# Merging 64-row tails into 128-row blocks and pinning TensorE to program order in a fused attention, Fourier-mixing and MLP kernel

## The chip, the cores and the metric

One core of a Trainium2 chip. The metric is device microseconds (us) of one execution. Every execution told of here was in the fast state (granted TensorE clock 0.968 to 0.985 over the whole span). Each variant ran four times, interleaved on the same chip with runs of the kernel before; different sets of variants ran on different chips, where the kernel before had medians of 1899.0 to 1903.5 us. Between sets, ratios compare better than medians. "Profile" and "trace" are one recorded execution of a kernel.

## The reference, cut to what matters

```python
def _attn_ref(q, k, v, tau):                       # q, k, v: (8, 8, 576, 64) fp32
    scores = np.matmul(q, k.transpose(0, 1, 3, 2)) / np.sqrt(64)
    thresh = np.max(scores, axis=-1, keepdims=True) - tau
    scores = np.where(scores >= thresh, scores, -1e9)
    attn = np.exp(scores - np.max(scores, axis=-1, keepdims=True))
    return np.matmul(attn / (attn.sum(-1, keepdims=True) + 1e-9), v)

def _moe_ref(x, w_ch1, w_ch2):                     # x: (8, 576, 512), the heads side by side
    u = x + np.real(np.fft.fft(np.fft.fft(x, axis=1), axis=2))
    un = (u - u.mean(-1)) / np.sqrt(u.var(-1) + 1e-6)          # cut: keepdims
    return u + np.maximum(un @ w_ch1, 0.0) @ w_ch2  # 512 -> 2048 -> 512
```

## The kernel before: the parts that matter

A batch is four pairs of heads. A pair is five steps of queries: four of 128 rows and a tail of 64 (576 = 4 x 128 + 64). A step computes scores (`sc`, two heads in the two row halves of the array), a reduction, an exponential and a masked product on VectorE and ScalarE, then transposes of the weights (`pw`) and of their last columns and the reciprocals (`pe`). After five steps `weighted_values` (`pv`) follows. Between these pieces `fill()` puts work of earlier batches: Fourier mixing (`py`, `pa`) and MLP (`ph`, `po`, `pn`). This filling is what keeps TensorE busy.

The "array shape" of a matmul is the part of TensorE's array that it uses, rows by columns; the traces print it, as 64*128 for scores or 128*128 for a full transpose. Two matmuls in a row with different ones make a "change of shape".

```python
ROWS = [128, 128, 128, 128, 64]
def prep_pair(n):                       # q and k of a pair to [head_dim, rows]
    for src, tag in ((qt, "qT"), (kt, "kT")):
        pt = ps.tile([128, 1024], FP32, tag="wide", bufs=3, name="pt")
        for t in range(NT):
            m = ROWS[t]
            nc.tensor.transpose(pt[:, 128 * t : 128 * t + m], src[0:m, t, :, :], ident[0:m, 0:m])
        # ... to qT on VectorE, to kT on ScalarE
def scores(i):
    sc = [ps.tile([128, 2, 512], FP32, tag="wide", bufs=3, name=f"sc{j}") for j in range(2)]
    for c in range(2):
        for j in range(2):
            hp = slice(64 * j, 64 * j + 64)
            nc.tensor.matmul(sc[j][0:m, c, 0:HALF], qT[hp, 128 * t : 128 * t + m],
                             kT[hp, HALF * c : HALF * (c + 1)], start=True, stop=True)
    # ... per head: neg (max), e (exp), e * (sc >= thr) with its sum; then rec = 1 / sum
def transposed_weights(i):
    pw = ps.tile([128, 8, 128], FP32, tag="wide", bufs=3, name="pw")   # 8 transposes of e
    nc.scalar.copy(e_t[:, :, qs], pw[:, :, 0:m])
    pe = ps.tile([128, 4, 128], FP32, tag="mm", name="pe")             # 2 transposes
    nc.scalar.copy(ends[:, :, qs], pe[:, 0:2, 0:m])
def weighted_values(n):
    for h in range(2):
        pv = ps.tile([128, 512], FP32, tag="mm", name="pv")            # 10 matmuls
        nc.vector.tensor_tensor(out=x[:, cols], in0=pv[:, 0:HALF], in1=ends[:, 1, cols], op=ALU.mult)
    # ... x, with two rows swapped by DMA, is folded on GpSimd: half, then f
    if n % NPAIR == 1:
        fold_chunks(b, 1)                                              # two sums of f on VectorE
# the loop
for i in range(total + 1):
    if i < total: scores(i)
    fill()
    if i > 0: transposed_weights(i - 1)
    if t == 3: prep_pair(n + 1)         # cut: not for the last pair
    fill()
    if i > 0 and t == 0: weighted_values(n - 1)
    # ... queue the mixing and the MLP groups of a finished batch
    fill()
for unit in mixes + [unit for _, unit in work]:
    for _ in unit: pass
```

PSUM has two kinds of buffers here: three "wide" ones of 1024 values a row (`sc`, `pt`, `pw`) and two small "mm" ones of 512 (`pe`, `pv`, `py`, `pa`, `ph`, `po`, `pn`). A scheduler orders each engine's instructions when the program is built; it may place a matmul ahead of another that was written earlier. "Pinning" below means that TensorE keeps the order of the program text instead.

Of the kernel before, what the change touches and what calls it, by code (L numbers as in the profile page):

```python
# [9 lines left out]
FP32 = mybir.dt.float32  # L10
INT32 = mybir.dt.int32
UINT32 = mybir.dt.uint32
ALU = mybir.AluOpType
ACT = mybir.ActivationFunctionType
# [33 lines left out]
def kernel(  # L48
# [12 lines left out]
    nc = tc.nc  # L61
# [2 lines left out]
    HID = w_ch1.shape[1]  # L64
    assert S == 576 and D == 64 and DM == 512 and H % 2 == 0
    NPAIR = H // 2
    ROWS = [128, 128, 128, 128, 64]
    NT = len(ROWS)
    ND = DM // 128
    NJ = HID // 128  # L70
    HALF = S // 2
# [38 lines left out]
    def load_pair(n):  # L110
        b, p = n // NPAIR, PAIRS[n % NPAIR]
        hs = [2 * p + (j + p) % 2 for j in range(2)]
        qt = sb.tile([128, NT, 2, D], FP32, tag="q", bufs=1, name="q_in")
        kt = sb.tile([128, NT, 2, D], FP32, tag="k", bufs=1, name="k_in")
        for j, h in enumerate(hs):
            nc.sync.dma_start(
                out=qt[:, 0:4, j, :], in_=q[b, h, 0:512, :].rearrange("(t p) d -> p t d", p=128)
            )
            nc.sync.dma_start(out=qt[0:64, 4, j, :], in_=q[b, h, 512:576, :])


        h = hs[0]
        nc.sync.dma_start(
            out=kt[:, 0:4, 0, :], in_=k[b, h, 0:512, :].rearrange("(t p) d -> p t d", p=128)
        )
        nc.sync.dma_start(out=kt[0:64, 4, 0, :], in_=k[b, h, 512:576, :])
        h = hs[1]
        nc.sync.dma_start(out=kt[0:64, 0, 1, :], in_=k[b, h, 512:576, :])
        rows = k[b, h, 0:512, :].rearrange("(t r p) d -> p r t d", r=2, p=64)
        nc.sync.dma_start(out=kt[64:128, 0:4, 1, :], in_=rows[:, 0])  # L130
        nc.sync.dma_start(out=kt[0:64, 1:5, 1, :], in_=rows[:, 1])
        loaded[n] = (qt, kt)

    def load_v(n):

# [189 lines left out]

    def prep_pair(n):

        qt, kt = loaded.pop(n)
        ts = []
        for src, tag in ((qt, "qT"), (kt, "kT")):  # L330
            pt = ps.tile([128, 1024], FP32, tag="wide", bufs=3, name="pt")
            for t in range(NT):
                m = ROWS[t]
                nc.tensor.transpose(  # L334
                    pt[:, 128 * t : 128 * t + m], src[0:m, t, :, :], ident[0:m, 0:m]
                )
            dst = sb.tile([128, S], FP32, tag=tag, name=tag)
            if tag == "qT":
                nc.vector.tensor_scalar(
                    out=dst[:, :], in0=pt[:, 0:S], scalar1=q_scale[:, :], scalar2=None, op0=ALU.mult  # L340
                )
            else:
                nc.scalar.copy(dst[:, :], pt[:, 0:S])
            ts.append(dst)
        heads[n] = (ts[0], ts[1], v_in[n % 2])
        if n + 1 < B * NPAIR:
            load_pair(n + 1)

    def scores(i):
        n, t = divmod(i, NT)  # L350
        qT, kT = heads[n][0:2]
        m = ROWS[t]
        sc = [ps.tile([128, 2, 512], FP32, tag="wide", bufs=3, name=f"sc{j}") for j in range(2)]
        for c in range(2):
            for j in range(2):
                hp = slice(64 * j, 64 * j + 64)
                nc.tensor.matmul(  # L357
                    sc[j][0:m, c, 0:HALF],
                    qT[hp, 128 * t : 128 * t + m],
                    kT[hp, HALF * c : HALF * (c + 1)],  # L360
                    start=True,
                    stop=True,
                )
        neg = sb.tile([128, 2], FP32, tag="neg", bufs=3, name="neg")
        thr = sb.tile([128, 2], FP32, tag="thr", bufs=3, name="thr")
        den = sb.tile([128, 2], FP32, tag="den", bufs=3, name="den")

        e = sb.tile([128, 2 * S], FP32, tag="e", name="e")
        for j in range(2):
            nc.vector.tensor_reduce(  # L370
                out=neg[0:m, j : j + 1], in_=sc[j][0:m, :, 0:HALF], axis=AXIS_XY, op=ALU.max,
                negate=True,
            )
        nc.vector.tensor_scalar(
            out=thr[0:m, :], in0=neg[0:m, :], scalar1=-1.0, scalar2=thr_off[0:m, :],
            op0=ALU.mult, op1=ALU.add,
        )
        for j in range(2):
            ej = e[0:m, S * j : S * (j + 1)].rearrange("p (c n) -> p c n", c=2)
            nc.scalar.activation(  # L380
                out=ej, in_=sc[j][0:m, :, 0:HALF], func=ACT.Exp, bias=neg[0:m, j : j + 1], scale=1.0
            )
            nc.vector.scalar_tensor_tensor(  # L383
                out=ej, in0=sc[j][0:m, :, 0:HALF], scalar=thr[0:m, j : j + 1], in1=ej,
                op0=ALU.is_ge, op1=ALU.mult, accum_out=den[0:m, j : j + 1],
            )
        nc.vector.tensor_scalar(
            out=den[0:m, :], in0=den[0:m, :], scalar1=1e-9, scalar2=None, op0=ALU.add
        )
        nc.vector.reciprocal(den[0:m, :], den[0:m, :])  # L390
        rec = sb.tile([128, 2 * D], FP32, tag="rec", name="rec")
        nc.gpsimd.tensor_copy(  # L392
            rec[0:m, :].rearrange("p (j d) -> p j d", j=2), _repeated(den[0:m, :], D)
        )
        steps[i] = (e, rec)

    def transposed_weights(i):
        n, t = divmod(i, NT)
        m = ROWS[t]
        e, rec = steps.pop(i)  # L400
        if t == 0:


            e_t = sb.tile([128, 8, S], FP32, tag="e_t", bufs=1, name="e_t")
            ends = sb.tile([128, 2, S], FP32, tag="ends", bufs=1, name="ends")
            vt = heads[n][2]
            if PAIRS[n % NPAIR] % 2:

                vt = sb.tile([128, 10, D], FP32, tag="vr", bufs=1, name="v_rev")
                src = heads[n][2]  # L410
                nc.gpsimd.tensor_copy(vt[:, :, 0:1], src[:, :, 0:1])
                last = src[:, :, D - 1 : D]
                down = bass.AP(
                    tensor=last.tensor, offset=last.offset,
                    ap=[list(last.ap[0]), list(last.ap[1]), [-1, D - 1]],
                )
                nc.gpsimd.tensor_copy(vt[:, :, 1:D], down)
            heads[n] = (*heads[n][0:2], vt, e_t, ends)
        e_t, ends = heads[n][3:5]
        qs = slice(128 * t, 128 * t + m)  # L420
        pw = ps.tile([128, 8, 128], FP32, tag="wide", bufs=3, name="pw")
        for j in range(2):
            for c in range(4):
                c0 = (S + D) * j + 128 * c
                nc.tensor.transpose(  # L425
                    pw[:, 4 * j + c, 0:m], e[0:m, c0 : c0 + 128], ident[0:m, 0:m]
                )
        nc.scalar.copy(e_t[:, :, qs], pw[:, :, 0:m])  # L428
        pe = ps.tile([128, 4, 128], FP32, tag="mm", name="pe")
        nc.tensor.transpose(pe[:, 0, 0:m], e[0:m, 512:640], ident[0:m, 0:m])  # L430
        nc.tensor.transpose(pe[:, 1, 0:m], rec[0:m, :], ident[0:m, 0:m])  # L431
        nc.scalar.copy(ends[:, :, qs], pe[:, 0:2, 0:m])  # L432

    def weighted_values(n):

# [68 lines left out]
    def mixing(b):  # L504
# [15 lines left out]
                out=out_, in0=in0, scalar=factor, in1=in1, op0=ALU.mult, op1=ALU.add  # L520
            )
        nc.vector.tensor_tensor(out=f[:, 0, O], in0=s01[:, 0, O], in1=s01[:, 1, O], op=ALU.subtract)
        yield 0
        yield 0

        COS = ((0, 0, 65), (1, 65, 129), (2, 129, 257))
        SIN = ((0, 0, 128), (3, 128, 256))
# [160 lines left out]
    total = B * per_batch  # L688
    groups = 0
    todo = 0.0  # L690
    for i in range(total + 1):
        if i < total:
            scores(i)
        fill()
        n, t = divmod(i, NT)
        if i > 0:
            transposed_weights(i - 1)
        if t == 3 and n + 1 < B * NPAIR:
            prep_pair(n + 1)
        fill()  # L700
        if i > 0 and t == 0:
            weighted_values(n - 1)
            if n + 1 < B * NPAIR:
                load_v(n + 1)
        for _ in itertools.islice(chunks, 2):
            pass
        if i == 2:
            load_dim()
            load_seq()
        if i > 0 and i % per_batch == 0:  # L710
            b = i // per_batch - 1
            mixes.append(mixing(b))
            todo += MIX
            while (groups + 1) * GT <= (b + 1) * S:
                work.append((b, channels(groups)))
                groups += 1
                todo += GROUP
            keep = 0.25 * GROUP
            per_slot = (todo - spent - keep) / (3 * per_batch)
            budget = spent  # L720
        fill()
    for unit in mixes + [unit for _, unit in work]:
        for _ in unit:
            pass


# [44 lines left out]
```

## Time and profile before

1902.98 us, median of three runs (1898.41 to 1903.65). I divide a trace into three stages, which the rest of the text uses: batch 0, to the first score matmul of batch 1; the middle, to the last weighted-values matmul; the drain, to the end.

| kernel before | us |
|---|---|
| span of the trace | 1898.7 |
| batch 0 / middle / drain | 197.8 / 1494.6 / 206.4 |
| TensorE / VectorE / ScalarE / GpSimd busy | 1813.0 / 890.6 / 610.4 / 280.5 |
| waits of TensorE after 260 us, sum | 21 |
| changes of shape in the middle | 620 |

The rows that carry the argument stand in the prediction below. One more, the chain of waits: followed back from the last instruction, it stays on TensorE for 84 of 100 parts of the span. Of VectorE's 163 us on it, 89 lie in batch 0 and 71 are spread over the middle.

```profile
PE 84%; DVE 9%; POOL 3%; ACT 1%; issue 1%; SPq 1%; DMA 1%; DVEq 0%; POOLq 0%; ACTq 0%
```

### The profile page before, as it was taken

To read this page: it belongs to the slowest core of one execution; us is meant where nothing else is said; L and a number is where in the kernel's file an instruction comes from. 1 tells how busy PE (TensorE), PEld (TensorE's weight loads), DVE (VectorE), ACT (ScalarE), POOL (GpSimd) and SP (SyncE) were. 2 spreads that over 40 slices of the span, in tenths; PEclk is the share of its full clock that TensorE was granted. 3 is DMA by queue.
4 is the path that set the end of the run, shared out by engine and by line. 5 is a ranking of instruction groups with operands and counts; after the bars stand their busy time and mean duration, and the time that the engine had idled before them with its cause. 6 is when DMAs were issued, how large, how long until landed. Compare 5 with 4: busy or idle time off the path is not lost.

```text
span 1898.7 us, 21358 instructions
## 1 busy us (share of the span) xinstructions
PE 1813.0 (95%) x7920; PEld 1012.1 (53%) x7920; DVE 890.6 (47%) x2072; ACT 610.4 (32%) x1110; POOL 280.5 (15%) x568
## 2 busy tenths in 40 slices
PE   6777899999999999999999999999999999999999
PEld 3444655555455555555555555555555555555454
DVE  6998745543343555553344445544333355541010
ACT  3555534233223334332223234322323233421010
POOL 4444111121101021102011021102011021101000
PEclk9876999999999999999999999999999999999999
DMA  5432100100001110110000110101000001000000
GB/s 154 128 113 81 32 18 15 37 24 7 19 25 26 29 26 14 31 31 7 19 24 13 30 26 14 34 22 25 13 23 20 22 23 25 1 12 6 11 6 17
DMA packets 129803, 57.00 MB, mean 30 GB/s; under 512 B 120642, under 2 KB 120643, under 8 KB 129700
## 3 DMA queue, kind: packets, MB, share of 16 engines
q1 hardware_dynamic: 129588, 55.38, 10.9%
q8 instruction: 63, 1.03, 0.2%
q14 instruction: 40, 0.33, 0.1%
q0 software_dynamic: 112, 0.26, 0.1%
HBM read 46.02 MB, written 9.44 MB: 29 GB/s over the span
## 4 chain that ended last, share of the span: by engine, by line
PE 84%; DVE 9%; POOL 3%; ACT 1%; issue 1%; SPq 1%; DMA 1%; DVEq 0%; POOLq 0%; ACTq 0%
PE po L645 27%; PE ph L624 25%; PE sc L357 11%; PE pv L446 9%; PE pw L425 6%; PE pt L334 2%; DVE neg L370 2%; DVE e L383 2%; PE py L533 1%; POOL u_t L572 1%; POOL u_t L576 1%; PE pe L430 1%; DVE stage L279 1%; PE pa L550 1%; PE pe L431 1%
## 5 line engine op out<-in xcount | busy, mean ns | idle before, releaser
L624 PE MATMUL ph<-u_t,w 128*128 128x384 f32 x1536 | 533.6, 496 | 10.2 <-POOL u_t L572 4.7
L645 PE MATMUL po<-w,h 128*128 128x512 f32 x1152 | 536.3, 603 | 0.0
L380 ACT ACTIVATE e<-sc,neg 128x576 f32<-128x576 f32 (+1 forms) x320 | 230.0, 740 | 598.7 <-DVE neg L370 598.5
L624 PEld LDWEIGHTS ph<-u_t,w 128*128 128x128 f32 x1536 | 282.1, 191 | 214.3 <-issue 23.7
L370 DVE TENSOR_REDUCE neg<-sc 128x1 f32<-128x576 f32 (+1 forms) x320 | 230.4, 750 | 308.0 <-PE sc L357 307.5
L645 PEld LDWEIGHTS po<-w,h 128*128 128x128 f32 x1152 | 204.8, 190 | 228.8 <-issue 225.1
L357 PE MATMUL sc<-kT,qT 64*128 64x288 f32 (+1 forms) x1280 | 268.7, 450 | 37.8 <-DVE e L383 16.9
L383 DVE SCALAR_TENSOR_TENSOR e<-sc,thr,e 128x576 f32<-128x576 f32 (+1 forms) x320 | 250.7, 814 | 31.9 <-ACT e L380 14.7
L357 PEld LDWEIGHTS sc<-kT,qT 64*128 64x128 f32 (+1 forms) x1280 | 133.8, 183 | 167.5 <-issue 87.8
L392 POOL COPY rec<-den 128x128 f32<-128x128 f32 (+1 forms) x160 | 49.7, 311 | 1127.5 <-DVE den L390 842.1
L428 ACT COPY e_t<-pw 128x1024 f32<-128x1024 f32 (+1 forms) x160 | 148.0, 925 | 145.5 <-PE pw L425 140.2
L425 PEld LDWEIGHTS pw<-ident,e 128*128 128x128 f32 (+1 forms) x1280 | 143.3, 146 | 70.9 <-issue 49.2
L425 PE MATMUL pw<-ident,e 128*128 128x128 f32 (+1 forms) x1280 | 166.3, 274 | 0.5 <-DVE e L383 0.3
L630 ACT ACTIVATE h<-ph 128x384 f32<-128x384 f32 x96 | 47.1, 490 | 331.3 <-PE ph L624 331.3
L632 DVE TENSOR_SCALAR h<-ph 128x384 f32<-128x384 f32 x96 | 53.3, 555 | 201.7 <-PE ph L624 201.5
L451 DVE TENSOR_TENSOR x<-pv,ends 128x288 f32<-128x288 f32 x64 | 29.3, 458 | 178.5 <-PE pv L446 178.5
L652 DVE SCALAR_TENSOR_TENSOR u<-po,rstd,u 128x512 f32<-128x512 f32 x36 | 27.0, 749 | 127.2 <-PE po L645 127.2
L446 PE MATMUL pv<-e_t,v_in 128*64 128x288 f32 x512 | 71.9, 417 | 0.0
L446 PE MATMUL pv<-e_t,v_rev 128*64 128x288 f32 x512 | 71.4, 418 | 0.2 <-ACT ends L432 0.2
L432 ACT COPY ends<-pe 128x256 f32<-128x256 f32 (+1 forms) x160 | 57.1, 357 | 0.9 <-PE pe L431 0.8
L446 PEld LDWEIGHTS pv<-e_t,v_in 128*64 128x64 f32 x512 | 35.6, 138 | 37.4 <-issue 7.4
L446 PEld LDWEIGHTS pv<-e_t,v_rev 128*64 128x64 f32 x512 | 35.4, 139 | 36.2 <-issue 10.5
(123 smaller groups left out, 1335.8 us busy)
## 6 DMA issues: line engine op xcount, KB each, us to landing
stage<-in_moe_w_ch_dram SPq DMA_DIRECT2D x32, 512.0 KB, 4.1
out_dram<-u SPq DMA_DIRECT2D x36, 256.0 KB, 2.0
q_in<-in_q_dram SPq DMA_DIRECT2D x64, 128.0 KB, 2.4
v_in<-in_v_dram SPq DMA_DIRECT2D x64, 128.0 KB, 2.4
k_in<-in_k_dram SPq DMA_DIRECT2D x32, 128.0 KB, 2.4
k_in<-in_k_dram SPq DMA_DIRECT2D x64, 64.0 KB, 2.3
q_in<-in_q_dram SPq DMA_DIRECT2D x64, 16.0 KB, 2.2
k_in<-in_k_dram SPq DMA_DIRECT2D x64, 16.0 KB, 2.1
```

The source lines that it names most:

```text
L357: nc.tensor.matmul(sc[j][0:m, c, 0:HALF], qT[hp, 128 * t : 128 * t + m], kT[hp, HALF * c : HALF * (c + 1)], start=True, stop=True,)
L370: nc.vector.tensor_reduce(out=neg[0:m, j : j + 1], in_=sc[j][0:m, :, 0:HALF], axis=AXIS_XY, op=ALU.max, negate=True,)
L380: nc.scalar.activation(out=ej, in_=sc[j][0:m, :, 0:HALF], func=ACT.Exp, bias=neg[0:m, j : j + 1], scale=1.0)
L383: nc.vector.scalar_tensor_tensor(out=ej, in0=sc[j][0:m, :, 0:HALF], scalar=thr[0:m, j : j + 1], in1=ej, op0=ALU.is_ge, op1=ALU.mult, accum ...
L392: nc.gpsimd.tensor_copy(rec[0:m, :].rearrange("p (j d) -> p j d", j=2), _repeated(den[0:m, :], D))
L425: nc.tensor.transpose(pw[:, 4 * j + c, 0:m], e[0:m, c0 : c0 + 128], ident[0:m, 0:m])
L428: nc.scalar.copy(e_t[:, :, qs], pw[:, :, 0:m])
L432: nc.scalar.copy(ends[:, :, qs], pe[:, 0:2, 0:m])
L446: nc.tensor.matmul(pv[64 * j : 64 * j + 64, 0:HALF], vt[:, 2 * c + j, :], e_t[:, 4 * j + c, cols] if c < 4 else ends[:, 0, cols], start=(c ...
L624: nc.tensor.matmul(ph[:, 0:GT], w1[c][:, 128 * j : 128 * (j + 1)], u_t[:, c, c0 : c0 + GT], start=(c == 0), stop=(c == ND - 1),)
L632: nc.vector.tensor_relu(ht, ph[:, 0:GT])
L645: nc.tensor.matmul(po[:, :], hT[j // 4][:, j % 4, 128 * t : 128 * (t + 1)], w2[j][:, :], start=(j == 0), stop=(j == NJ - 1),)
```

## The change

Two intents. First, put the two 64-row tails of q and k into one 128-row block, and the tail's queries of both heads into one 128-row step (head 0 in rows 0 to 63, head 1 in 64 to 127), so that VectorE and ScalarE do one full operation where they did two half-filled ones, and TensorE has no 64-row transposes. Second, stop the scheduler from reordering TensorE from the second batch on, so that both heads' score matmuls stay together. With it, one `fill()` moves ahead of `weighted_values`, the mixing waits one more step, and the end of the program keeps mixing and MLP interleaved.

```diff
-        qt = sb.tile([128, NT, 2, D], FP32, tag="q", bufs=1, name="q_in")
-        kt = sb.tile([128, NT, 2, D], FP32, tag="k", bufs=1, name="k_in")
+        qk = sb.tile([128, 9, 2, D], FP32, tag="qk", bufs=1, name="qk_in")
 ...                                       # block 8: q tail in rows 0-63, k tail in 64-127
+        for t in range(5):
+            nc.tensor.transpose(pq[:, 128 * t : 128 * t + 128], qk[:, t if t < 4 else 8, :, :], ident[:, :])
+        nc.vector.tensor_copy(kT[:, 512:S], pq[:, S : S + 64])
+        for t in range(4):
+            nc.tensor.transpose(pk[:, 128 * t : 128 * t + 128], qk[:, 4 + t, :, :], ident[:, :])
 ...                                       # scores of the tail: one tile for both heads
+            for j, c, c0, k0, w in (
+                (0, 0, 0, 0, HALF), (1, 0, 0, 64, HALF), (0, 1, 0, HALF, HALF),
+                (1, 1, 0, 64 + HALF, 512 - HALF), (1, 1, 512 - HALF, 0, 64),
+            ):
+                nc.tensor.matmul(sc[0][hp, c, c0 : c0 + w], qT[hp, 512:S], kT[hp, k0 : k0 + w], ...)
 ...                                       # mixing
-        yield 0
-        yield 0
+        for _ in range(3):
+            yield 0
 ...                                       # the loop
+        if i == per_batch:
+            ordered.enter_context(tc.manual_schedule(engines={mybir.EngineType.PE}))
 ...
         fill()
-        if i > 0 and t == 0:
-            weighted_values(n - 1)
 ...
+        fill()
+        if i > 0 and t == 0:
+            weighted_values(n - 1)
 ...
-    for unit in mixes + [unit for _, unit in work]:
-        for _ in unit:
-            pass
+    per_slot = GROUP / 32
+    while mixes or work:
+        fill()
```

> **What bounds the kernel now.** I read the page from the top, then the waits of TensorE, then its timeline in the middle, because a change of its order can only pay where TensorE is the bound.
>
> ```profile
> PE 1813.0 (95%) x7920; PEld 1012.1 (53%) x7920; DVE 890.6 (47%) x2072; ACT 610.4 (32%) x1110; POOL 280.5 (15%) x568
> PE   6777899999999999999999999999999999999999
> DVE  6998745543343555553344445544333355541010
> PEclk9876999999999999999999999999999999999999
> ```
>
> Batch 0 (the first four slices, 190 us) has nothing to fill TensorE with: VectorE is at 9 tenths, TensorE at 7, its clock sinks to 7 tenths. After that TensorE is full. (The list of waits of TensorE from 260 us on, columns: microseconds, times, longest.)
>
> ```profile
> PE ph L624 <- POOL u_t L572: 4.7, 3, 1.6
> PE sc L357 <- ACT e_t L428: 4.1, 5, 0.9
> PE pa L550 <- ACT tmp L565: 3.5, 4, 1.7
> PE pe L430 <- ACT tmp L565: 2.5, 3, 0.8
> PE ph L624 <- DVE h L632: 2.3, 6, 0.6
> ```
>
> All waits after 260 us sum to 21 us. So faster helpers buy nothing in the middle; only less TensorE time does, and new waits cost their full length. What TensorE's time is made of shows in the timeline (start, length, line, records; a matmul of fp32 leaves two records, a transpose one; read starts, as ends overlap):
>
> ```profile
> 911.47 2.85 PE L624 MATMUL ph<-u_t,w 128*128 128x384 f32 x8
> 914.15 1.04 PE L425 MATMUL pw<-ident,e 128*128 128x128 f32 x8
> 915.03 0.27 PE L430 MATMUL pe<-ident,e 128*128 128x128 f32 x1
> 915.13 0.27 PE L431 MATMUL pe<-ident,rec 128*128 128x128 f32 x1
> 915.25 0.80 PE L334 MATMUL pt<-ident,q_in 128*128 128x128 f32 x5
> 915.98 0.86 PE L334 MATMUL pt<-ident,k_in 128*128 128x128 f32 x5
> ...
> 973.87 1.24 PE L357 MATMUL sc<-kT,qT 64*128 64x288 f32 x8
> 975.04 3.70 PE L645 MATMUL po<-w,h 128*128 128x512 f32 x8
> ...
> 1090.33 0.75 PE L357 MATMUL sc<-kT,qT 64*128 64x288 f32 x2
> 1091.01 0.64 PE L533 MATMUL py<-dim_s,f 128*48 128x128 f32 x4
> 1091.58 0.75 PE L357 MATMUL sc<-kT,qT 64*128 64x288 f32 x2
> ```
>
> Three readings. (1) A 128-wide transpose costs (915.03-914.15)/8 = 0.11 us, a 64-row one about 0.062 (the tail's starts in the trace); but five of prep with one 64-row one cost 915.98-915.25 = 0.73 us, not 4x0.11+0.06 = 0.50: each change of the array's shape is paid. Where single records can be told apart, the last one before a change is 0.094 us longer and the first after it 0.104 longer: 0.20 us a change. (2) A whole score step (8 records, both heads in turn) costs 975.04-973.87 = 1.17 us, that is 4x0.243 for pairs that run together plus one 0.20. (3) One matmul of it alone, two records, costs 1091.01-1090.33 = 0.68 us: 2x0.243 plus 0.20. A step cut into single pieces thus runs its heads one after the other and pays the change each time. The scheduler cut many like that, because it starts a head when its PSUM buffer comes free.
>
> **What the Trainium skill says.** TensorEngine Tiling (Array Packing), Key Properties: "Changing tiling mode (not just tile) drains the TensorE", and tiles run independently. The trace agrees: 0.20 us a change, two heads at the price of one. TensorE: Matmul & The Clock Gate, Part 3: matmuls start and end in program order; so a matmul that waits holds all behind it. VectorE: DVE Perf Modes, Why tensor_reduce can't reduce along partition axis: each of the 128 partitions is an independent pipeline. So half-filled tails should cost as much as full ones, and the trace has the reduction at 752 ns for 128x576 and 744 ns for 64x576.
>
> **The change part by part.** I counted over the listing of the built programs' instruction order, between the first score of batch 1 and the last weighted value (4283 matmuls before, 4166 after).
>
> *Tails merged.* Prep: 10 transposes with two shape changes in and out become 9 of one shape. The tail's queries: 8+2 transposes of 64 rows become 4+2 of 128: 8x0.062 = 0.50 against 4x0.11 = 0.44, and two more 0.05 for the ends: nothing. The gain is the changes of shape: the list before has 620 in the middle; with the 64-row transposes counted as full ones it has 473. 147x0.20 = 29 us. The tail's scores stay 64x64 tiles: five matmuls for four, the piece of 64 columns costs about 0.11 us x28 = 3 us more; the ends 28x2x0.047 = 3 us more. VectorE loses a reduction (744), a masked product (807) and its accumulator read (83) for each of 32 tails, 1.63 us each, 52 us; ScalarE an exponential, 736x32 = 24 us; GpSimd gains a copy of 64 columns, and VectorE one for kT, about 0.15 us (the 2-column additions of this kernel take 0.155). In the middle those engines have slack: worth nothing. In batch 0, where VectorE bounds, four tails give 4x1.5 = 6 us at most; I take 4.
>
> *TensorE in program order.* Changes of shape fall from 473 to 342: 131x0.20 = 26 us. Score matmuls that run alone fall from 92 to none (the 64-column pieces aside): 46 pairs at 0.97 become 0.485: 22 us. The drain at the end keeps its work (ph 82.6 us, po about 102).
>
> TensorE time saved: 29+26+22-3-3 = 71 us, and 4 in batch 0: 75.
>
> *What program order costs.* The scheduler dodged buffers that were not yet free; a fixed order stops. I laid the durations along both listed orders and asked, for each use of a PSUM buffer, whether the former user can have been emptied. Times needed after the last matmul, from the trace: ends 1.4 us (the 1.01 us copy of pw is ahead of its 0.38), pw 1.27, pv 0.70, ph 0.76, py 0.87, scores 2.85 (0.75 reduction twice, threshold, masked product 0.82).
> The order before comes out 12 us short in sum, of the size of the buffer waits measured. The order after comes out 57 us short:
> - pv after pv, 14 times, 10 us: an output tile (po) stays open across many fills and holds one of two small buffers, so both halves share the other.
> - the ends' buffer taken at once by ph, pa or py: 34 times, 28 us.
> - ph after ph, 20 times, 6 us; prep after scores or pw, 9 times, 9 us; the rest 4 us.
> That is 45 us more. In the mixing, work also comes earlier than its inputs: in batches 1, 2, 4, 6 and in the last drain ph follows the last pa directly, while GpSimd still has about six additions of 0.7 us to do: about 4 us each, 20 us, where the waits before have 7. Against it: where one wait is served, the next is often covered; I take off 10. Net new waits: 45+13-10 = 48 us.
>
> Sum: 1903 - 75 + 48 = 1876; I put it at 1874, as an extra step of delay before the mixing starts should spare a little.
>
> **The rivals.** (a) New waits eat all: in-order stops of 75 us or more, and 1903 stays. For it: the list above counts only direct shortages and takes ScalarE and VectorE as idle when called, while they are busy 32% and 47%. Against: softmax itself has room, the median from the end of scores to their transposes is 11.5 us in the new order, only 2 of 141 under 3.2. It would give 1890 to 1915. (b) The waits hardly come: the shortages are hidden by the weight loads' lead and by matmuls that wait inside the 0.16 us tail of the one before; then the 71 us show, 1825 to 1845. For it: the order before, too, was predicted with shortages and its waits are short ones. Against: pv after pv and ends after ends have no slack at all. (c) Softmax on VectorE was the limit, and the saved 52 us count in full: against it stand 21 us of waits in 1640, and VectorE at 47%. It would give the same 1830, with the gain in VectorE's rows. (d) q and k share one single-buffered input tile now: prep waits for transfers. Landing takes 2.4 us and about ten issues 6 us, with five steps of 8 to 13 us between: hidden.
>
> **Range and chances.** Savings are countable and I trust them to 10 us; the waits are 48 give or take 30. So 1874, 8 in 10 within 1838 to 1914. Faster by over 2% means under 1865, a little above a third: 0.38. Slower by over 2%, over 1941, needs waits of over 110 us: 0.04. The rest, 0.58, stays within 2%.
>
> **What would show it.** TensorE's busy time falls from 1813 to about 1740 and matmul rows of scores lose most: from 269 us to about 235. No score line in the timeline has two records alone after 260 us; no transposes of 64 rows. The waits of TensorE after 260 us rise from 21 to 60 or 80 us, with pe, pv, pa, py and ph released by ScalarE's copies and GpSimd's u_t. VectorE falls by about 50 us. If waits stay under 35 us, rival (b) holds; if TensorE's busy time stays over 1780, a change of shape costs less than I read; if waits pass 100 us, (a). A first batch that ends later, or a drain longer than 206 us, would be a step I left out.

## The result, and the profile after

The kernel after took 1886.68 us (1884.89 to 1887.61, four runs) against 1903.24 (1898.41 to 1903.65, four runs) for the kernel before beside it: ratio 0.9918, 95% interval 0.9900 to 0.9936, within 2%. A ratio here is the mean time of one kernel's fast runs over the mean of the other's fast runs of the same rounds, so it is not quite the ratio of the medians.

The page of the kernel after, its busy times and three rows of slices:

```profile
PE 1752.9 (93%) x7824; PEld 1002.1 (53%) x7824; DVE 840.7 (45%) x2008; ACT 591.1 (31%) x1110; POOL 288.6 (15%) x600
PE   5777899999999999999999999999999998998999
DVE  6989644533333544453333444443334444521010
PEclk9877999999999999999999999999999999999999
```

TensorE lost 60 us of busy time, VectorE 50 us; yet the span fell only from 1898.7 to 1885.6. Two late slices show an eight, which none did before after the start: from 1556 to 1603 us, where a stop of 4.2 us lies that is followed up below, and from 1697 to 1744 us in the drain. The waits of TensorE after 260 us (us, times, longest):

```profile
PE ph L649 <- ACT ends L453: 15.2, 7, 4.2
PE pv L471 <- DVE x L476: 8.1, 14, 0.6
PE ph L649 <- POOL u_t L597: 8.0, 4, 2.8
PE pq L336 <- ACT e_t L441: 6.0, 5, 1.3
PE py L558 <- ACT ends L453: 4.0, 6, 1.2
PE pa L575 <- ACT ends L453: 3.7, 6, 1.1
```

The whole list has 62.4 us in 78 waits, where the list before has 21.4 us in 30. They are of the kinds the prediction named: a small PSUM buffer that ScalarE has not yet emptied, the second `pv` half behind the first, and MLP work whose input GpSimd still adds.

The timeline of TensorE shows what was bought:

```profile
688.36 0.77 PE L336 MATMUL pq<-ident,qk_in 128*128 128x128 f32 x5 [1.28 <-ACT e_t L441]
688.97 0.60 PE L344 MATMUL pk<-ident,qk_in 128*128 128x128 f32 x4
689.40 2.75 PE L649 MATMUL ph<-u_t,w 128*128 128x384 f32 x8
692.08 1.19 PE L371 MATMUL sc<-kT,qT 64*64 64x288 f32 x10
...
700.05 1.24 PE L360 MATMUL sc<-kT,qT 64*128 64x288 f32 x8
701.22 1.24 PE L649 MATMUL ph<-u_t,w 128*128 128x384 f32 x3
```

From start to start, the nine transposes of prep take 689.40-688.36 = 1.04 us without a change of shape, and a score step of both heads 701.22-700.05 = 1.17 us; no score matmul stands alone. But the prep also waited 1.28 us for its buffer, which the scheduler used to dodge.

To see where it went, I laid the durations read from the trace, with 0.20 us a change of shape, along the order in which the built programs list TensorE's instructions. That gives the middle without any stop ("listed"). The difference to the measured middle is called "stops": it holds the idle time that the list of waits shows, and all else that the durations leave out. The clock is not in it: from 260 to 1680 us it was granted at 1.00 in both traces.

| us | before | after | difference |
|---|---|---|---|
| batch 0, measured | 197.8 | 190.7 | -7.1 |
| middle, listed | 1464.2 | 1391.0 | -73.2 |
| middle, stops (measured less listed) | 30.4 | 91.0 | +60.6 |
| drain, measured | 206.4 | 212.9 | +6.5 |
| span | 1898.7 | 1885.6 | -13.1 |

Changes of shape fell from 620 to 342, and score matmuls that run alone from 92 to none. So by this listing TensorE's work shrank by 73 us, and four fifths of it came back as stops.

How far one trace can be trusted shows in drain_b below, whose built program has the same instructions in the same order on every engine as the kernel after, up to the last weighted values. Its batch 0 was 3.1 us shorter, and the stretch from there to step 40 1.9 us longer; from step 40 to step 140 ("six batches") both took 1130.6 us. So differences of 2 or 3 us in batch 0 or the whole middle say nothing, and six batches are the better ruler.

### The profile page after: what moved, and what is told of

It is laid out like the page before. It is cut to its first block, busy times and chain, and to the rows that moved or that the text cites. A ratio compares the mean times of both kernels' runs of the same rounds, so it can differ in the third digit from the quotient of the medians.

```text
span 1885.6 us, 21229 instructions
## 1 busy us (share of the span) xinstructions
PE 1752.9 (93%) x7824; PEld 1002.1 (53%) x7824; DVE 840.7 (45%) x2008; ACT 591.1 (31%) x1110; POOL 288.6 (15%) x600
## 5 line engine op out<-in xcount | busy, mean ns | idle before, releaser
L649 PE MATMUL ph<-u_t,w 128*128 128x384 f32 x1536 | 532.9, 497 | 29.1 <-ACT ends L453 15.2
L392 ACT ACTIVATE e<-sc,neg 128x576 f32<-128x576 f32 x288 | 206.6, 741 | 634.7 <-DVE neg L382 634.6
L382 DVE TENSOR_REDUCE neg<-sc 128x1 f32<-128x576 f32 x288 | 206.7, 752 | 305.9 <-PE sc L360 239.0
L395 DVE SCALAR_TENSOR_TENSOR e<-sc,thr,e 128x576 f32<-128x576 f32 x288 | 226.9, 815 | 41.0 <-ACT e L392 26.6
L360 PE MATMUL sc<-kT,qT 64*128 64x288 f32 x1024 | 187.0, 447 | 28.5 <-DVE e L395 17.1
L404 POOL COPY rec<-den 128x128 f32<-128x128 f32 x160 | 49.6, 310 | 913.6 <-DVE den L402 757.5
L441 ACT COPY e_t<-pw 128x1024 f32<-128x1024 f32 x128 | 129.3, 1011 | 128.0 <-PE pw L440 127.9
L360 PEld LDWEIGHTS sc<-kT,qT 64*128 64x128 f32 x1024 | 103.3, 194 | 121.0 <-issue 76.1
L440 PEld LDWEIGHTS pw<-ident,e 128*128 128x128 f32 x1024 | 123.2, 146 | 50.4 <-issue 39.6
L440 PE MATMUL pw<-ident,e 128*128 128x128 f32 x1024 | 142.1, 284 | 0.0
L283 POOL TENSOR_TENSOR w<-w,stage 128x512 f32<-128x512 f32 x32 | 45.9, 1434 | 57.7 <-DVE stage L279 39.8
```

The lines of the kernel that those rows point to most:

```text
L360: nc.tensor.matmul(sc[j][:, c, 0:HALF], qT[hp, 128 * t : 128 * t + 128], kT[hp, HALF * c : HALF * (c + 1)], start=True, stop=True,)
L382: nc.vector.tensor_reduce(out=neg[:, j : j + 1], in_=sc[j][:, :, 0:HALF], axis=AXIS_XY, op=ALU.max, negate=True,)
L392: nc.scalar.activation(out=ej, in_=sc[j][:, :, 0:HALF], func=ACT.Exp, bias=neg[:, j : j + 1], scale=1.0)
L395: nc.vector.scalar_tensor_tensor(out=ej, in0=sc[j][:, :, 0:HALF], scalar=thr[:, j : j + 1], in1=ej, op0=ALU.is_ge, op1=ALU.mult, accum_out ...
L404: nc.gpsimd.tensor_copy(rec[:, :].rearrange("p (j d) -> p j d", j=nh), _repeated(den[:, 0:nh], 2 * D // nh))
L440: nc.tensor.transpose(pw[:, 4 * j + c, :], e[:, c0 : c0 + 128], ident[:, :])
```

## The experiments

Theory A (mine): the merge pays by removing changes of shape; pinning TensorE pays about 48 us in listed work and loses about as much in stops, each at a place where a buffer or an input is not ready. Rivals: B, the merge pays because it relieves VectorE; C, the stops come from the moved fills and the new drain and not from pinning; D, pinning pays once the few bad stops are removed.

All twelve kernels gave correct results. The edits are against the kernel after unless said otherwise.

### merge_bare: the merge alone

```diff
-            ordered.enter_context(tc.manual_schedule(engines={mybir.EngineType.PE}))
# and the loop, the two yields and the end of the program as in the kernel before
```

> Tails merged, the scheduler left free, loop and fills as before. Theory (changes of the array's shape are paid 0.20 us each, and the scheduler's order has few waits): the listed order has 471 changes of shape in batches 1 to 7 for 620, so about 27 us of TensorE time less, 7 us less in batch 0 (VectorE), waits of TensorE after 260 us stay near 20 us; about 1870 us, faster than the full change by some 15 us. Rival (the merge is worth little, the gain of the change came from the order): within 6 us of 1903.

Measured: 1863.87 us, ratio 0.9794 (0.9779 to 0.9808). Batch 0, middle, drain 184.6, 1470.1, 206.4. Half of the change is better than the whole. The listed middle fell to 1438.2, so 26 us of listed work, and the waits stayed at 18.8 us:

```profile
PE ph L649 <- POOL u_t L597: 3.6, 3, 1.2
```

No wait for `ends`, none of `pv`. That fits theory A, but does not part it from B: of the 37.6 us by which the span fell, 24.5 are in the middle, near the listed 26, and 13.2 are in batch 0, where VectorE is busier than TensorE (170 and 147 of the first 200 us before).

### order_only: pinning, fills and drain, with the tails as before

```diff
# the kernel before, with manual_schedule from the second batch on, three yields,
# the fill() moved ahead of weighted_values and the new loop at the end
```

> Tails as before; TensorE in program order from batch 1 on, with the moved fills and the new drain. Theory: 492 changes of shape for 620 (25 us less) and no score matmul alone (22 us less), but 50 to 65 us of new stops, as the waits on the ends' buffer, pv and u_t do not depend on the merge: 1905 to 1920 us, waits after 260 us of 60 to 75 us. Rival (the order is what pays, the stops come from the merge): under 1890 us with waits under 40.

Measured: 1915.92 us, ratio 1.006 (1.0043 to 1.0077): a little slower than before. Waits 64.2 us in 75, the same heads of the list as after (`ph` for `ends` 15.2, `pv` for x 8.1). The listed time of six batches (from step 40 to step 140) fell from 1126.6 to 1093.1 us, and the measured one rose from 1141.8 to 1149.3. Theory A held on this point: pinning, moved fills and new drain together lose.

### pv_wide: both halves of the weighted values in one wide buffer

```diff
+        both = ps.tile([128, 2, 512], FP32, tag="wide", bufs=3, name="pv")
         for h in range(2):
-            pv = ps.tile([128, 512], FP32, tag="mm", name="pv")
+            pv = both[:, h, :]
```

> The changed kernel, with both halves of the weighted values in the two banks of one of the wide PSUM tiles in place of the small ones. Theory (pv waits for pv because an open po holds the other small buffer): the 14 waits of pv for DVE x vanish, 8 us by the list of waits and 10 us counted from start to start, so 1876 to 1880 us. Rival (a wait removed is only passed on to the next one in order, here to scores that now find one wide tile less): 1884 to 1890 us.

Measured: 1897.26 us, ratio 0.9966 (0.9951 to 0.9981), worse than after. A miss of the experiment's design:

```profile
PE pv L472 <- DVE x L477: 16.4, 27, 0.7
```

The wait it should have removed doubled, from 14 times to 27. The two halves lie apart in the buffer, but they are one tile, and the second half now waited for the reading of the first in nearly all pairs. It shows nothing of the theories, but that sharing a tile is a dependency of its own.

### pv_two_wide: each half its own wide buffer

```diff
-            pv = ps.tile([128, 512], FP32, tag="mm", name="pv")
+            pv = ps.tile([128, 1024], FP32, tag="wide", bufs=3, name="pv")
```

> The changed kernel, with each half of the weighted values in a wide PSUM tile of its own. In the run before, one tile for both made every second half wait for the first one's reader (27 waits in place of 14). Theory: no wait of pv for DVE x is left, 8 to 10 us less, about 1877 us. Rival (it only moves to scores and prep, which then lack two wide tiles): waits of sc or pq rise by 5 us or more and the time stays over 1883.

Measured: 1867.24 us, ratio 0.9823 (0.9808 to 0.9838), ten us better than expected. The waits of `pv` are gone from the list, and the middle fell by 7.3 us, close to their 8.1. The rest is batch 0 (182.2 against 190.7) and the drain (-3.1). In batch 0 TensorE is not pinned, and the scheduler did choose otherwise: the built program has 47 changes of shape there for 55. That this gives the 8.5 us is not shown.

### fold_late: the two sums of the fold one pair later

The longest stop is 4.2 us, three times. Its chain in the kernel after, in order of time:

```profile
716.42 1.13 SPq L485 DMA_DIRECT2D x<-swap  x2
...
719.46 1.54 POOL L495 TENSOR_TENSOR half<-x 128x287 f32<-128x287 f32 x2
720.96 1.83 POOL L499 TENSOR_TENSOR f<-half 128x143 f32<-128x143 f32 x4
...
722.90 0.20 POOL L508 TENSOR_TENSOR f<-x 128x2 f32<-128x2 f32 x1
...
723.14 0.79 DVE L519 TENSOR_TENSOR sums<-f 128x608 f32<-128x608 f32 x1 [3.61 <-POOL f L508]
...
724.67 1.42 DVE L382 TENSOR_REDUCE neg<-sc 128x1 f32<-128x576 f32 x2
725.46 0.74 ACT L392 ACTIVATE e<-sc,neg 128x576 f32<-128x576 f32 x1 [3.89 <-DVE neg L382]
726.10 1.00 ACT L441 COPY e_t<-pw 128x1024 f32<-128x1024 f32 x1
...
727.62 0.38 ACT L453 COPY ends<-pe 128x256 f32<-128x256 f32 x1
...
728.06 4.54 PE L649 MATMUL ph<-u_t,w 128*128 128x384 f32 x8 [4.16 <-ACT ends L453]
```

Read from the bottom: `ph` needs the small buffer that `pe` holds; ScalarE copies it out late, because in its queue the exponential of the next step stands ahead; that waits for the reduction; and the reduction stands behind a sum on VectorE that idles 3.61 us for GpSimd's fold of x, which a DMA had to deliver first. The Trainium skill says it of the queues (PSUM — Partial Sum Buffer, Engine vs sequencer instructions): "ScalarE/VectorE/GpSimdE queues are strict FIFO." This trace agrees: the scores of the reduction were done by about 722.2 us, and it started at 724.67, after the two sums. So a wait that the list puts down to ScalarE comes, in part, from VectorE's queue, four instructions further back.

```diff
-        if n % NPAIR == 1:
+        if n % NPAIR == 2:
```

> The changed kernel, with the sums of the first two chunks of a batch issued one pair later. Theory (VectorE, which takes its queue in order, stands on that sum for 3.6 us, waiting for GpSimd, and holds up the softmax, the exponentials ahead of the copies in ScalarE's queue, and with them the small buffer that ph needs): the three waits of ph for the ends of 4.2 us go, that group falls from 15 us to under 4, and the time to about 1874 us. Rival (the copies are late because ScalarE's queue is long anyway): the group stays over 10 us.

Measured: 1885.65 us, ratio 0.9902 (0.9887 to 0.9917), no effect. The scheduler, which still orders VectorE, took the sums back to the same place: the trace has them there with the same 3.61 us. The test failed, not the theory.

### fold_pool: the two sums on GpSimd

```diff
-            fold_chunks(b, 1)
+            fold_chunks(b, 1, nc.gpsimd)
-    def fold_chunks(b, c):
-        nc.vector.tensor_tensor(...)
+    def fold_chunks(b, c, eng=nc.vector):
+        eng.tensor_tensor(...)
```

> The changed kernel, with the sums of the first two chunks of a batch done by GpSimd itself, right behind its own work. The run before this one left VectorE's order as it was, as the scheduler pulled the sums forward again. Theory (VectorE waiting in order for GpSimd holds up the softmax, then ScalarE's copies, then ph's buffer): the three waits of ph of 4.2 us go, ph for the ends falls from 15 us to under 4, the time to about 1874 us. Rival (ScalarE's queue is long anyway): the group stays over 10 us and the time over 1883.

Measured: 1873.02 us, ratio 0.9852 (0.9836 to 0.9869). The waits of `ph`:

```profile
PE ph L649 <- ACT ends L453: 7.9, 7, 1.7
...
724.87 2.85 PE L649 MATMUL ph<-u_t,w 128*128 128x384 f32 x8 [1.75 <-ACT ends L453]
```

The second row, from the timeline, is the matmul that had waited 4.16 us. It and the two others like it now wait 1.75 us each, 2.4 to 2.5 less, as much as the reduction had been late; here the reduction starts when its scores are done. Six batches fell by 8.1 us (1130.6 to 1122.5), the waits of this group by 7.3. So the chain above is shown to cause 2.4 us of each 4.2 us stop. The other 1.75 us stay, and with them the group keeps more than the 4 us I expected.

### drain_b: the last part to the scheduler and in the old sequence

```diff
-    per_slot = GROUP / 32
-    while mixes or work:
-        fill()
+    ordered.close()
+    for unit in mixes + [unit for _, unit in work]:
+        for _ in unit:
+            pass
```

> The changed kernel, with the last part after the last batch left to the scheduler and in the old sequence. Theory (the drain grew by 6.5 us because in order the last filler is used up before the sums of the mixing, so that ph stands waiting for GpSimd): the stretch from the last weighted value to the end falls from 212.9 to about 206.5 us, the rest stays, about 1880 us. Rival (the drain is longer only because work was shifted into it): it stays over 210.

Measured: 1882.98 us, ratio 0.9906 (0.9892 to 0.9921). The drain fell from 212.9 to 207.1, which is the 6.5 us that the change had added, within 0.7. The middle rose by 3.7 and batch 0 fell by 3.1, most of it with the same instructions, as said above, so that the total does not show the drain's 5.8 us cleanly. The edit does two things, the old sequence and the release to the scheduler. The table of order_free and order_bare below has the drain at 210.0 us with the new sequence and the scheduler free, and 212.9 with it pinned, so each gives about half. The lines of the drain, first of the kernel after, then of before:

```profile
1704.84 1.56 PE L649 MATMUL ph<-u_t,w 128*128 128x384 f32 x4
...
1709.23 7.18 PE L649 MATMUL ph<-u_t,w 128*128 128x384 f32 x12 [2.84 <-POOL u_t L597]
```

```profile
1710.07 0.41 PE L554 MATMUL pa<-seq_xo,y_e 128*1 128x144 f32 x2
1710.41 14.00 PE L645 MATMUL po<-w,h 128*128 128x512 f32 x32
1724.25 5.97 PE L624 MATMUL ph<-u_t,w 128*128 128x384 f32 x18
```

Before, 14 us of finished-input work (`po`) lay between the last mixing matmul and the MLP group that needs GpSimd's sums. In the kernel after that work had been spent earlier, and `ph` followed the mixing at once.

### combo: the three repairs together, and MLP units ahead of the mixing unit in a fill

```diff
# pv_two_wide + fold_pool + drain_b, and in fill():
+        while work and spent < budget and work[0][0] < mixed:   # before "if mixes:", not after it
```

> The three edits together, and in each fill the work units ahead of the mixing unit, so that a mixing matmul does not take the ends' buffer at once. Theory (the stops are separate and add up): 12+9+6 us and about 5 more less than 1886, so 1852 to 1860 us, just under the merge alone with the scheduler free (1864). Rival (stops in order replace each other): over 1868.

Measured: 1838.12 us, ratio 0.9672 (0.9657 to 0.9687), 14 us below the low end expected. Middle 1446.0, waits 34.8 us in 59. So repaired, the pinned kernel beats the merge alone. Which share the reordered fill has beside the three repairs was not run apart. That looked like D; the next run decides it.

### combo_free: the same without pinning

```diff
-            ordered.enter_context(tc.manual_schedule(engines={mybir.EngineType.PE}))
+            pass
```

> The run of the three edits together, with TensorE's order left to the scheduler. Theory (program order pays once its stops are gone: 332 changes of shape for 426 and no score matmul alone for 50, 35 us by the listed orders, against some 25 us more of stops): this is slower than the ordered one by about 10 us, 1845 to 1856 us. Rival (the edits, not the order, made it fast): 1838 us or less.

Measured: 1835.79 us, ratio 0.9657 (0.9638 to 0.9676), against combo's 0.9672 (0.9657 to 0.9687): the intervals overlap, a tie. It is the fastest kernel of the study, 3.4% under the kernel before. Waits 9.2 us in 21. In six batches:

| six batches, us | listed | measured | stops | changes of shape |
|---|---|---|---|---|
| combo | 1073.8 | 1104.2 | 30.3 | 238 |
| combo_free | 1098.6 | 1103.8 | 5.2 | 308 |

Pinning saves 25 us of listed work and costs 25 us of stops. My expectation of 1845 to 1856 was wrong; D fell. The repairs help the scheduler's version as well.

### pad_tails: the kernel before with its tails only filled up

```diff
# against the kernel before: GpSimd zeroes rows 64 to 127 of the tails, of e and of rec, and
-                    pt[:, 128 * t : 128 * t + m], src[0:m, t, :, :], ident[0:m, 0:m]
+                    pt[:, 128 * t : 128 * t + 128], src[:, t, :, :], ident[:, :]
# likewise for pw and pe
```

> The kernel before, with the 64-row tails only padded: GpSimd sets their upper halves to zero and they are transposed as full 128-row blocks; nothing is merged, VectorE and ScalarE work as before. Theory (what the merge saves in the middle is changes of the array's shape at 0.20 us, not work): 459 changes for 620 and fewer cut score steps, against transposes that are 0.047 us longer each: by the listed order 19 us less between batch 1 and the last weighted value, which takes 1475 us for 1495; batch 0 stays over 192 us, since VectorE is not relieved; about 1884 us. Rival (fewer instructions on VectorE and ScalarE were the gain): the middle is no shorter, 1900 us or more.

Measured: 1889.13 us, ratio 0.9943 (0.9915 to 0.9971). It removes the changes of shape (620 to 459 in the middle) without taking any reduction or exponential away: VectorE keeps its 320 reductions. The middle fell by 6.1 us, where its listed time fell by 18.8. In six batches it is 9.1 of 15.6 us; around the start of batch 1 some 6 us more went where the granted clock was 0.50. So the changes of shape do pay by themselves. This run also makes the 64-row transposes as long as full ones and adds memsets.

Part of what is missing is the price in the listing. Read again from start to start, two changes around a whole score step cost 0.40 us (in the kernel after, 42 steps between two `ph` or two `po`), but around a run of 64-row transposes in the kernel before only 0.34 us, and 0.29 where full transposes follow. With these prices six batches should fall by 12.5 us here, where 9.1 was measured, and by 17.5 us in merge_bare, where 18.1 was measured. So in the middle the count of TensorE's own work accounts for the merge's gain and leaves little to B. In batch 0, which holds a third of the merge's gain, A and B are not parted.

### order_free and order_bare: pinning and the loop taken apart

After merge_bare one thing was open: whether the pinning or the moved fills bring the stops (rival C). order_free is the kernel after with the scheduler free; order_bare is merge_bare with TensorE pinned.

```diff
# order_free, against the kernel after
-            ordered.enter_context(tc.manual_schedule(engines={mybir.EngineType.PE}))
+            pass
# order_bare, against merge_bare
+        if i == per_batch:
+            ordered.enter_context(tc.manual_schedule(engines={mybir.EngineType.PE}))
+    ordered.close()                      # ahead of the units at the end
```

> The changed kernel with its moved fills, its third step of delay and its new drain loop, but with TensorE's order left to the scheduler throughout. Theory (pinning TensorE is what brings the stops): the scheduler dodges the occupied buffers again, so waits of TensorE after 260 us fall under 25 us, and the time is near that of the merge alone, 1862 to 1872 us. Rival (the moved fills and the new drain bring them): waits stay over 45 us and the time over 1880. The drain stays over 210 us if its loop is what lengthens it.

> The merge alone, with TensorE in program order from the second batch to the last weighted values, fills where they were before, the old drain. Theory: pinning alone takes some 30 us off the listed work of six batches and gives as much or more back in stops: 1872 to 1890 us, waits after 260 us 50 us or more, drain near 206. Rival: program order suits the old placement of the fills better, and the time falls under 1860.

Measured, all four with merged tails:

| | us (median) | ratio | middle | drain | waits after 260 us |
|---|---|---|---|---|---|
| merge_bare: free, fills as before | 1863.87 | 0.9794 | 1470.1 | 206.4 | 18.8 |
| order_bare: pinned, fills as before | 1900.47 | 0.9997 | 1502.8 | 207.4 | 72.8 |
| order_free: free, fills moved, new end | 1860.03 | 0.9781 | 1459.1 | 210.0 | 19.2 |
| after: pinned, fills moved, new end | 1886.68 | 0.9918 | 1482.0 | 212.9 | 62.4 |

The heads of the lists of waits, first of order_bare, then of order_free:

```profile
PE py L558 <- ACT ends L453: 11.3, 6, 2.6
PE ph L649 <- DVE h L657: 8.4, 12, 1.4
PE pv L471 <- DVE x L476: 8.1, 14, 0.6
```

```profile
PE ph L649 <- POOL u_t L597: 7.5, 4, 2.2
```

(merge_bare ran on another chip than order_bare and order_free; the kernel before took 1903.52 us there and 1902.42 us here.) Rival C fell: with the fills moved and the scheduler free the waits are 19 us; pinning alone brings them to 62 or 73. Pinning costs 36.6 us of median time with the old fills and 26.7 with the moved ones. Moving the fills helps both ways, more under pinning (13.8 us) than without (3.8), although with the new end the drain is 3.6 us longer (206.4 to 210.0 with the scheduler free). order_bare came out 10 us slower than the range I gave: the stops it gained in six batches (17.6 to 69.6 us, 52 us) exceed the 30 us that it saved in listed work by more than I had thought.

## Why the prediction was right, and where it was not

The time, 1886.68, lies in the range of 1838 to 1914 and in the likeliest class, and the mechanism stands: TensorE's work shrinks by some 70 us as listed, and stops give most of it back. The point, 1874, was 12.7 us too low. By its own steps:

- **TensorE's time saved.** 71 us predicted in the middle, 73.2 in the listed order after. The two halves: merging 29-3-3 = 23 predicted, 1464.2-1438.2 = 26.0 listed, and a middle 24.5 us shorter measured in merge_bare; order 26+22 = 48 predicted, 1438.2-1391.0 = 47.2 listed. The listing uses the prediction's own 0.20 us, so it checks the counts and not the price. That price is too high for the 64-row transposes: the prediction's own row has 0.73-0.50 = 0.23 us for the two changes of a prep, not 0.40, and the trace 0.29 to 0.34 with the matmul that follows. So the 29 us for 147 changes are about 5 us too many. Score matmuls took 227.9 us of TensorE after 268.7, where about 235 was predicted. Right but for these 5 us.
- **TensorE's busy time.** 1740 predicted, 1752.9 measured. Stops rose by 40.2 us in six batches (15.2 to 55.4), shown idle by 26.9 (15.9 to 42.8); the difference stays in "busy". A part of it is the way a wait is recorded: a transpose's record lasts 0.27 us, where the next one can start after 0.11, so 0.16 us of a wait behind it count as busy.
- **Net new waits, 48 us.** This is the term that was mis-sized. The stops rose by 60.6 us in the middle, 12.6 more than taken. The list of waits rose by 41 us, inside the 60 to 80 us in all that I named, and its kinds came near or under their price: for the ends' buffer 25.6 us in 22 waits (28 in 34 named), `pv` 8.1 (10), prep 6.6 (9), `ph` for GpSimd 8.0 (20). What I had not added is what the list does not show, some 20 us of the 60.6. As estimates, 48 more waits at 0.16 us are 8 of these, and the too high price of the 64-row transposes, which makes the stops before look smaller, is 4 or 5; the rest is open. Nor had I foreseen that a queue makes some waits longer: I took ScalarE and VectorE as idle when called, and 2.4 us of each of the three 4.2 us stops come from a softmax that stood behind a sum that waited.
- **The drain, "keeps its work".** It does, but it took 6.5 us longer, as the work that used to cover GpSimd's additions had been used up earlier. I had priced about 4 us for it among the mixing inputs, and that the whole drain would stay the same was wrong.
- **Batch 0, 4 us.** 7.1 us in the kernel after, and 13.2 in merge_bare, 10.4 in order_free, 12.6 in order_bare. More than the bound of 6 that I gave from VectorE's operations. Of this, 3 us are no more than the spread between executions: the kernel after, drain_b and order_free have the same batch 0 and took 190.7, 187.6 and 187.4 us for it. Which placement in batch 0 gives which time is open; the granted clock there also differs (0.69 before and 0.81 after from 150 to 200 us).
- **Rivals.** (a), stops of 75 us or more, did not come, though 60.6 and the drain come near. (b) fell with the waits of 62 us. (c), VectorE as the limit in the middle: VectorE lost the 50 us foreseen, and order_bare, where it lost 43 (847.5 us busy), gains nothing; so VectorE's relief by itself does not set the time. (d) stayed hidden: of prep's waits the long ones name `e_t`, not a transfer.

A total inside the range hides two errors of opposite sign. By parts the prediction had the merge at 23+4 = 27 us and the order at 48-48 = 0, with 2 us of rounding on top. In medians the merge gave 1903.24-1863.87 = 39.4 us, and the rest of the change took back 1886.68-1863.87 = 22.8. So the second half of the change is a loss as a whole. The loss is the pinning: without it, and with the moved fills kept, order_free took 1860.03 us.

## What to carry to other kernels

When TensorE is full, count its changes of array shape and its half-occupied tiles: that work is real and can be counted before anything runs. Pinning an engine's order sells the scheduler's freedom to go round a buffer that is not yet free; price each place where a tile follows its former user, with the queues of the engines that empty it, before expecting a gain. Test the parts of a change alone even when the whole is a gain: here the merge alone gained more than twice as much as the whole (39.4 us for 16.6).

## What the Trainium skill lacked or had wrong

- TensorEngine Tiling (Array Packing), Key Properties, says that a change of tiling mode drains TensorE and gives no size. Here it is 0.20 us a change at score steps (0.094 us on the last record before it, 0.104 on the first after it) and 0.15 to 0.17 around 64-row transposes, 620 changes in the middle before, 8% of that stage.
- Perfetto Trace Analysis, Tensor Engine Instruction (MATMUL, LD_WEIGHTS), says that the end of a matmul is estimated. It does not say what follows for waits: idle time before a matmul can be shown too short. Here, in six batches, stops grew by 40.2 us where shown idle grew by 26.9.
- No page that I read weighs a pinned order of TensorE against a scheduler's: 62 to 73 us of waits pinned without repairs, against 19 to 21 us free.
